# The second batch's chain: its products put behind the second-layer product of the moment and asked for later

## The chip, the cores and the metric

One core of a Trainium2 chip runs the whole kernel. The metric is the device time of one execution in microseconds. Three runs of the kernel before took 738.49, 745.61 and 740.89 us, median 740.89.

## What is computed

Four batches of 11,456 tokens of width 128 go through agent attention with 49 agents and then through a mixture of eight experts. Cut to what matters:

```python
a2k = sm(agents, k)                 # 49 agents over all keys, scaled softmax
agent_v = a2k @ v                   # per batch: 49 x 128
q2a = sm(q, agents)                 # every token over the 49 agents
x = q2a @ agent_v                   # attention output, 45824 x 128

xn = x / (norm(x) + 1e-6); en = expert_emb / (norm(expert_emb) + 1e-6)
logits = xn @ en.T / tau            # tau = 0.1
e = argmax(logits); gate_w = softmax(logits)[e]
out = gate_w * (relu(x @ w1[e]) @ w2[e])     # F = 1024 hidden units
```

## The kernel before, in words

Keys of a batch are read in blocks of 1,024 tokens, scored against the agents (tile `sp`), and the exponentials weight the values (`avp`). That gives the agents' values for the batch, and from them one expert that nearly all of the batch's tokens go to. With only 49 agent vectors behind every token, the kernel multiplies the agents' values into that expert's first layer once (`gp`), ranks the 1,024 hidden units, places the few that are not plainly linear into a small pair of weight matrices (`gh`, `gl` for the first layer, `w2p` for the second), and folds the rest into one linear matrix `lin`. Tokens that this doesn't cover are found by the products `vp` and mended later.

The piece from the agents' values to these small matrices is **the batch's chain**: `av_chain` (product `foldp`, its copy `lr` and `avT`, a sum over squares by the product `total<-avsq`, the router's weights `rp` rounded into `r_hi` and `r_lo`) and, started from it, `pick_expert` (product `key`, from which VectorE makes the expert's number `e0i`; SyncE reads it and loads the expert's weights `w1s` and `w2s`; ScalarE squares them, L688, and `total<-wsq` sums; then `gp`, the gates `gts`, the key of each hidden unit, the product `row`, ranks, the 0/1 matrices `sel`, the products `placed`, `linp` and `w2pp`, two products `mT` and `mB` for a maximum over partitions, the threshold `thr`).

While the chain of one batch goes on, the tokens of the batch before go through their layers, unit by unit: tokens are transposed on TensorE (`fTp`), scored (`sp`), routed (`rtp`), and in `route_group` get their gate `gs`. `ffn_mm1` is the first layer (`hp`, rectified into `hh`), and some ticks later `ffn_mm2` the second: it opens an accumulator `yp` with the linear part (`yp<-lin`, L1192) and adds the hidden units (`yp<-w2f`, L1201, or `yp<-w2p`, L1204 to L1206). `yp` has two accumulators; `ffn_out` frees one by writing `ot`, which is `yp` times `gs` (L1220, on VectorE). Scores, routing and the chain's products share another two (`pss`).

The kernel is written as generators: a `yield n` lets n half steps of other work be recorded before the generator goes on. A scheduler then sets each engine's order from dependencies and priorities. `in_place(last)` tells it that an instruction has to stand behind a named one. `y_last` is the last product of the second layer so far, so `in_place(y_last)` puts a product into TensorE's queue behind that. `gp`, `rp` and `placed` had it before. SyncE's queue keeps the order of the program, and the read of the expert's number holds it until the number is there.

Of the kernel before, what the change touches and what calls it, by code (L numbers as in the profile page):

```python
# [29 lines left out]
def kernel(ctx: ExitStack, tc: tile.TileContext, q, k, v, agents, emb, tau, w1, w2, out):  # L30
# [11 lines left out]
    AT = {2: {0: 0, 2: 1}, 3: {0: 0, 1: 1, 3: 2}}  # L42
    KEEP = 5
    LATE = 13

# [162 lines left out]

    def allmax(col, n, tag, psx, g, bufs=2):

        t_ = psx("mT")
        pe.transpose(out=t_[:n, :P], in_=col, identity=ident)
        mx = sm.tile([P, 1], F32, name="mTx", tag="mTx")[:n]
        dve.tensor_reduce(out=mx, in_=t_[:n, :P], axis=AX.X, op=ALU.max)
        yield g
        t_ = psx("mB")
        pe.matmul(out=t_[:, :n], lhsT=mx.broadcast_to([n, P]), rhs=ident[:n, :n], start=True, stop=True)
# [30 lines left out]

    def total(col, psx):

        s = psx("total")[:, :1]
        pe.matmul(out=s, lhsT=ones, rhs=col, start=True, stop=True)
        return s
# [294 lines left out]
    def av_chain(b, g):  # L548
        bt = batches[b]
        while not ready:  # L550
            yield 1
        psx = pss if ffn_at[0] else psy
        s = psx("foldp")
        fm = [(kb.x, kb.fold) for kb in bt.blks]
        for i, (x, m) in enumerate(fm):
            pe.matmul(out=s[:, :A], lhsT=x[:, :D], rhs=m, start=(i == 0), stop=(i == len(fm) - 1))
        for i, (x, m) in enumerate(fm):
            pe.matmul(out=s[:, LO : LO + A], lhsT=x[:, D : D + 1].broadcast_to([P, D]), rhs=m, start=(i == 0), stop=(i == len(fm) - 1))
        lr = sm.tile([P, A], F32, name="lr", tag="lr")
# [22 lines left out]
        if b == 0:  # L582
            rp, i = routing()
            p_last.append(i)
        bt.sg, bt.isg = yield from half_scale(total(sq, psx), 7, "sg")
        sg2 = sm.tile([P, 1], F32, name="sg2", tag="sg2")
# [41 lines left out]
    def pick_expert(b, g):  # L628
# [8 lines left out]
        sav = sm.tile([P, 1], F32, name="sav", tag="sav")  # L637
        dve.tensor_reduce(out=sav, in_=bt.avT[:, :A], axis=AX.X, op=ALU.add)
        key = psx("key")[:, :E]
        pe.matmul(out=key, lhsT=sav.broadcast_to([P, P]), rhs=enT, start=True, stop=True)  # L640
        km = sm.tile([P, 1], F32, name="km", tag="km")
# [45 lines left out]
        with in_place(q_last if b == 0 else h_last):  # L687
            act.activation(junk[0], w1s, AF.Square, accum_out=sq[0])  # L688
        s2, i2 = yield from half_scale(total(sq[0], psx), 2, "w1")
        sgw = sm.tile([P, 1], F32, name="sgw", tag="sgw")  # L690
# [7 lines left out]
        def second():  # L698

            act.activation(w2x[:, :, 0], w2s, AF.Square, accum_out=sq[1])  # L700
            s3, i3 = yield from half_scale(total(sq[1], psx), 6, "w2")
            yield g
            act.activation(w2x[:, :, 0], w2s, AF.Copy, scale=s3)
            if b > 0:
                pool.tensor_tensor(out=w2s, in0=w2s, in1=s3.unsqueeze(2).broadcast_to([P, NF, D]), op=ALU.mult)
                pool.tensor_tensor(out=w2x[:, :, 1], in0=w2s, in1=w2x[:, :, 0], op=ALU.subtract)
            return s3, i3
# [26 lines left out]
        if b > 0:  # L734
            s3, i3 = yield from second()
        yield g
        for h in range(2):
            t_ = psx("row")
            hs = slice(h * 512, h * 512 + 512)
            pe.matmul(out=t_, lhsT=ones, rhs=diag.rearrange("p c f -> p (c f)")[:, hs], start=True, stop=True)  # L740
            act.copy(row[:, hs], t_)
            yield g
# [24 lines left out]
        gmx = sm.tile([P, 2], F32, name="gmx", tag="gmx")  # L767
        yield 2 * g
        act.copy(gh, placed(0, FM))
# [19 lines left out]
        for h in (1, 0):  # L789
            vec.tensor_tensor(out=gts[:, :, h, :A], in0=ga, in1=mask.unsqueeze(2).broadcast_to([P, NF, A]), op=ALU.mult)  # L790
        yield 3 * g
        t_ = psx("linp")
        for c in range(NF):
            pe.matmul(out=t_[:, :D], lhsT=gts[:, c].rearrange("p h a -> p (h a)"), rhs=w2s[:, c],
                      start=(c == 0), stop=(c == NF - 1))
        ls_ = s3 if b == 0 else 1.0
# [6 lines left out]
        for f in range(0, NM, 2):  # L803
            t_ = psx("w2pp")
            nk = min(2, NM - f)
            for k_ in range(nk):
                for c in range(NF):
                    pe.matmul(out=t_[:, k_ * 2 * D : (k_ + 1) * 2 * D], lhsT=sel[:, c, (f + k_) * P : (f + k_ + 1) * P],
                              rhs=w2x[:, c].rearrange("p h d -> p (h d)"), start=(c == 0), stop=(c == NF - 1))
            (act.copy if f % 4 else dve.tensor_copy)(w2p[:, f : f + nk].rearrange("p f h d -> p (f h d)"), t_[:, : nk * 2 * D])  # L810
            yield g
# [7 lines left out]
        yield 1  # L819
        top = yield from allmax(gmx, 2, "gmxr", psx, 1)  # L820
        thr = sm.tile([P, 1], F32, name="thr", tag="thr")
# [4 lines left out]
        for c in range(NF):  # L826
            dve.tensor_scalar(sel[:, c, :FV], iotaf[:, :FV], rank[:, c : c + 1], sgn[:, c : c + 1], ALU.is_equal, ALU.mult)
            if c % 4 == 3:
                yield g
        yield 3 * g  # L830
        t_ = placed(0, FV)
# [845 lines left out]
```

## Time and profile before

| | before |
|---|---|
| median of three runs | 740.89 us |
| the profiled execution | 741.78 us |
| its span | 740.0 us |
| mean granted clock of TensorE | 0.972 |
| TensorE busy | 688.6 us |
| VectorE busy | 568.1 us |
| ScalarE busy | 475.6 us |
| GpSimd busy | 338.8 us |

The span is what the trace covers; the execution's own time is 1.8 us longer. Busy shares are means over the whole run, so the table alone tells only that TensorE has little room. Where the room lies, the windows and the timelines below show. The clock is given as a share of full speed.

### The profile page before, as it was taken

The page shows a single profiled execution, that of the slowest core. Times are in us where ns is not written, and L with a number is a line of the kernel's source. Part 1 is how long each engine was busy: PE and PEld are TensorE (multiplying, and loading weights), DVE is VectorE, ACT ScalarE, POOL GpSimd, SP SyncE. Part 2 cuts the span into 40 slices and gives each one's busy share as a digit, 9 for nine tenths or more (in the row PEclk, how much of TensorE's full clock was granted, in tenths as well). Part 3 has the DMA queues.
Part 4 walks back from the last instruction along what each step waited for, and adds up shares of the span by engine and source line. Part 5 has one row for each costly group of instructions (what it writes and reads, how often), then busy time and mean ns, then how long its engine had stood idle before and what let it go on. Part 6 is the DMA issues. An engine that isn't in the chain of part 4 may idle for free.

```text
span 740.0 us, 23507 instructions
## 1 busy us (share of the span) xinstructions
PE 688.6 (93%) x9416; PEld 574.9 (78%) x9416; DVE 568.1 (77%) x1499; ACT 475.6 (64%) x1161; POOL 338.8 (46%) x576
## 2 busy tenths in 40 slices
PE   8997889989978899999999889989999999999996
PEld 6886678867867788788888778878897776787675
DVE  4676887864457999988558998965658899789886
ACT  3436858667457757877758837865669447766772
POOL 5003401572245557655615836565638356255410
PEclk9998999999969999999999999999999999999998
DMA  8986239846389786598659439945452247223211
GB/s 329 278 306 215 94 73 249 187 137 197 95 205 342 154 199 166 148 279 214 160 158 268 112 67 253 287 124 159 135 172 94 81 87 194 62 60 115 61 45 64
DMA packets 157817, 122.59 MB, mean 166 GB/s; under 512 B 78727, under 2 KB 134105, under 8 KB 157707
## 3 DMA queue, kind: packets, MB, share of 16 engines
q1 hardware_dynamic: 144331, 97.44, 51.1%
q10 hardware_dynamic: 13120, 23.47, 9.1%
q8 instruction: 74, 1.21, 0.7%
q14 instruction: 36, 0.29, 0.1%
q0 software_dynamic: 256, 0.17, 0.1%
HBM read 79.14 MB, written 23.72 MB: 139 GB/s over the span
## 4 chain that ended last, share of the span: by engine, by line
PE 56%; DVE 23%; DMA 6%; ACT 5%; issue 4%; POOL 4%; SPq 0%; ACTq 0%; POOLq 0%; DVEq 0%
PE sp L430 8%; PE fTp L417 6%; PE avp L521 6%; PE hp L1168 4%; PE hp L1169 4%; PE yp L1192 3%; PE yp L1201 3%; DVE hh L1178 3%; PE yp L1204 3%; PE yp L1206 3%; PE yp L1205 3%; PE vp L1017 3%; DMA kt<-in_k_dram 2%; DVE ot L1220 2%; DMA xq<-in_q_dram,ix 1%
## 5 line engine op out<-in xcount | busy, mean ns | idle before, releaser
L1026 ACT ACTIVATE vp<-vp 128x512 f32<-128x512 f32 x191 | 112.3, 588 | 31.7 <-PE vp L1014 16.3
L1178 DVE SCALAR_TENSOR_TENSOR hh<-hp,hh 128x512 f16<-128x512 f32 (+1 forms) x147 | 98.4, 675 | 24.5 <-ACT hh L1177 23.9
L1204 PE MATMUL yp<-w2p,hh 128*128 128x128 f16 (+1 forms) x582 | 109.9, 220 | 0.0
L1205 PE MATMUL yp<-w2p,hh 128*128 128x128 f16 (+1 forms) x582 | 109.8, 220 | 0.0
L1206 PE MATMUL yp<-w2p,hh 128*128 128x128 f16 (+1 forms) x582 | 108.5, 220 | 0.0
L1177 ACT ACTIVATE hh<-hp 128x512 f16<-128x512 f32 (+1 forms) x147 | 85.1, 587 | 34.9 <-PE hp L1169 28.7
L430 PEld LDWEIGHTS sp<-aT_all,fT 128*64 128x64 f32 (+1 forms) x2400 | 83.7, 140 | 23.2 <-issue 11.5
L430 PE MATMUL sp<-aT_all,fT 128*64 128x49 f32 (+1 forms) x2400 | 97.6, 228 | 3.8 <-DVE qe L874 1.4
L1168 PE MATMUL hp<-tt,gh 128*128 128x512 f16 (+1 forms) x207 | 77.5, 377 | 4.3 <-DVE fT L420 2.4
L1169 PE MATMUL hp<-tt,gl 128*128 128x512 f16 (+1 forms) x207 | 77.8, 378 | 0.0
L965 POOL TENSOR_TENSOR nrm<-qq,half 128x16 f32<-128x16 f32 (+2 forms) x28 | 70.4, 2515 | 0.3
L884 POOL TENSOR_TENSOR e<-qe,e 128x392 f16<-128x392 f32 (+1 forms) x44 | 38.1, 866 | 68.0 <-ACT e L881 67.8
L1220 DVE TENSOR_TENSOR ot<-yp,gs 128x512 f32<-128x512 f32 (+1 forms) x92 | 61.1, 670 | 9.3 <-PE yp L1206 3.7
L1201 PE MATMUL yp<-w2f,hh 128*128 128x128 f32 (+1 forms) x456 | 66.7, 284 | 0.0
L1192 PE MATMUL yp<-lin,tt 128*128 128x128 f16 x720 | 63.3, 221 | 2.9 <-DVE w2p L810 1.4
L1204 PEld LDWEIGHTS <-hh 128*128 128x128 f16 (+1 forms) x582 | 57.6, 99 | 10.3 <-issue 0.5
L422 ACT COPY fT<-fTp 128x512 f32<-128x512 f32 (+1 forms) x87 | 48.6, 563 | 24.7 <-PE fTp L417 17.9
L1206 PEld LDWEIGHTS <-hh 128*128 128x128 f16 (+1 forms) x582 | 57.5, 99 | 8.1 <-issue 1.5
L1205 PEld LDWEIGHTS <-hh 128*128 128x128 f16 (+1 forms) x582 | 57.4, 99 | 5.8 <-issue 0.3
L1201 PEld LDWEIGHTS yp<-w2f,hh 128*128 128x128 f32 (+1 forms) x456 | 58.9, 194 | 2.9 <-issue 1.1
L926 POOL TENSOR_TENSOR rt<-rt 128x384 f32<-128x384 f32 (+1 forms) x48 | 40.5, 843 | 45.1 <-DVE rt L923 42.0
L417 PE MATMUL fTp<-ident,qt 128*128 128x128 f32 x360 | 57.0, 288 | 3.3 <-ACT fT L422 1.1
(373 smaller groups left out, 1786.3 us busy)
## 6 DMA issues: line engine op xcount, KB each, us to landing
kt<-in_k_dram SPq DMA_DIRECT2D x44, 512.0 KB, 6.6
vt<-in_v_dram SPq DMA_DIRECT2D x44, 512.0 KB, 6.2
qt<-in_q_dram SPq DMA_DIRECT2D x44, 512.0 KB, 5.5
out_dram<-ot ACTq DMA_DIRECT2D x88, 256.0 KB, 3.4
w1s<-in_moe_w_dram SPq DMA_DIRECT2D x8, 512.0 KB, 4.6
w2s<-in_moe_w_dram SPq DMA_DIRECT2D x8, 512.0 KB, 5.6
tt<-e SPq DMA_TRANSPOSE x44, 4.1
kt<-in_k_dram SPq DMA_DIRECT2D x4, 96.0 KB, 5.8
```

The lines of the kernel that those rows point to most:

```text
L417: pe.transpose(out=tp[:, c * p : (c + 1) * p], in_=src[:p, c0 + c, :], identity=ident[:p, :p])
L430: pe.matmul(out=s[h : h + w, c * A : (c + 1) * A], lhsT=xT[:, c * p + h : c * p + h + w], rhs=aT_all[:, b, :], start=True, stop=True, skip ...
L1026: act.activation(z[:p], z[:p], AF.Relu, scale=-1.0, accum_out=bt.vsum[:p, at : at + 1])
L1168: pe.matmul(out=hp[:, :m], lhsT=bt.gh[:, fs], rhs=tt, start=True, stop=False)
L1169: pe.matmul(out=hp[:, :m], lhsT=bt.gl[:, fs], rhs=tt, start=False, stop=True)
L1177: h_last[:] = [act.activation(hh[:, :m], hp[:, :m], AF.Relu)]
L1178: dve.scalar_tensor_tensor(out=hl[:, :m], in0=hp[:, :m], scalar=0.0, in1=hh[:, :m], op0=ALU.max, op1=ALU.subtract)
L1192: pe.matmul(out=yp[:p, c, :], lhsT=tc_, rhs=bt.lin[:, h], start=(c == 0 and h == 0), stop=False, skip_group_check=True)
L1201: y_last[:] = [pe.matmul(out=y, lhsT=hh[:, cs], rhs=bt.w2f[:, f], start=False, stop=last, skip_group_check=True)]
L1204: pe.matmul(out=y, lhsT=hh[:, cs], rhs=wh, start=False, stop=False, skip_group_check=True)
L1205: pe.matmul(out=y, lhsT=hh[:, cs], rhs=wl, start=False, stop=False, skip_group_check=True)
L1206: y_last[:] = [pe.matmul(out=y, lhsT=hl[:, cs], rhs=wh, start=False, stop=last, skip_group_check=True)]
```

## The change

A constant `EASY = 1` names the second batch. For that batch's chain alone, `foldp`, the three sums `total`, `key`, `row`, `linp`, `w2pp`, `mT` and `mB` are issued in place behind the second-layer product of the moment, and before several of them (and before `placed`) two or three more half steps are let pass. Nothing else is added, and no instruction is removed. Lines move down by up to 23.

```diff
+    EASY = 1
...
     def allmax(col, n, tag, psx, g, bufs=2, b=None):
...
+        with on_time(b):
+            pe.transpose(out=t_[:n, :P], in_=col, identity=ident)
...
-        yield g
+        yield g + (b == EASY)
...
+    def on_time(b):
+
+        return in_place(y_last) if b == EASY else nullcontext()
+
-    def total(col, psx):
+    def total(col, psx, b=None):
 
         s = psx("total")[:, :1]
-        pe.matmul(out=s, lhsT=ones, rhs=col, start=True, stop=True)
+        with on_time(b):
+            pe.matmul(out=s, lhsT=ones, rhs=col, start=True, stop=True)
...
         psx = pss if ffn_at[0] else psy
+        if b == EASY:
+            yield 2
         s = psx("foldp")
...
-        bt.sg, bt.isg = yield from half_scale(total(sq, psx), 7, "sg")
+        if b == EASY:
+            yield 3
+        bt.sg, bt.isg = yield from half_scale(total(sq, psx, b), 7, "sg")
...
+        if b == EASY:
+            yield 2
         key = psx("key")[:, :E]
-        pe.matmul(out=key, lhsT=sav.broadcast_to([P, P]), rhs=enT, start=True, stop=True)
+        with on_time(b):
+            pe.matmul(out=key, lhsT=sav.broadcast_to([P, P]), rhs=enT, start=True, stop=True)
...
-        s2, i2 = yield from half_scale(total(sq[0], psx), 2, "w1")
+        if b == EASY:
+            yield 3
+        s2, i2 = yield from half_scale(total(sq[0], psx, b), 2, "w1")
...
-            s3, i3 = yield from half_scale(total(sq[1], psx), 6, "w2")
+            if b == EASY:
+                yield 3
+            s3, i3 = yield from half_scale(total(sq[1], psx, b), 6, "w2")
...
-        yield g
+        yield g + 2 * (b == EASY)
         for h in range(2):
             t_ = psx("row")
...
-        yield 2 * g
+        yield 2 * g + 2 * (b == EASY)
         act.copy(gh, placed(0, FM))
...
-        yield 3 * g
+        yield 3 * g + 2 * (b == EASY)
         t_ = psx("linp")
...
-        top = yield from allmax(gmx, 2, "gmxr", psx, 1)
+        top = yield from allmax(gmx, 2, "gmxr", psx, 1, b=b)
...
-        yield 3 * g
+        yield 3 * g + 2 * (b == EASY)
         t_ = placed(0, FV)
```

`foldp`, `row`, `linp` and `w2pp` are wrapped in `on_time(b)` in the same way.

What moves is seen in each engine's order. **SyncE's queue around the read of the expert's number** of the second batch, before:

```order
L161 DMA qt<-in_q_dram 128x1024
L161 DMA kt<-in_k_dram 128x1024
L837 TENSOR_LOAD e0i
...
L840 DMA w1s<-in_moe_w_dram 128x1024
...
L841 DMA w2s<-in_moe_w_dram 128x8x128
L161 DMA qt<-in_q_dram 96x256
L481 DMA_TRANSPOSE kT<-ks 128x16x128
L161 DMA kt<-in_k_dram 128x1024
L161 DMA qt<-in_q_dram 128x1024
```

and with the change:

```order
L162 DMA qt<-in_q_dram 128x1024
L162 DMA kt<-in_k_dram 128x1024
L162 DMA qt<-in_q_dram 96x256
L489 DMA_TRANSPOSE kT<-ks 128x16x128
L162 DMA kt<-in_k_dram 128x1024
L860 TENSOR_LOAD e0i
...
L863 DMA w1s<-in_moe_w_dram 128x1024
...
L864 DMA w2s<-in_moe_w_dram 128x8x128
L162 DMA qt<-in_q_dram 128x1024
```

The last block of queries, the transpose of a key block and a load of keys, which stood behind the two loads of the expert's weights, now stand ahead of the read.

**TensorE from the folding product to the first batch's next second-layer product**, before (products that only repeat, and those of other work between, are left out):

```order
L556 MATMUL foldp<-fold,avx 128x49
L558 MATMUL foldp<-fold,avx 128x49
L252 MATMUL total<-avsq,ones 128x1
L640 MATMUL key<-enT,sav 128x8
...
L579 MATMUL rp<-enT,avT 128x8
L580 MATMUL rp<-avT 128x49
L430 MATMUL sp<-aT_all,fT 64x49 x32
L252 MATMUL total<-wsq_3572,ones 128x1
...
L682 MATMUL gp<-avT,w1s 128x49 x8
...
L1192 MATMUL yp<-lin,tt 128x128
...
L1201 MATMUL yp<-w2f,hh 128x128 x4
```

and with the change:

```order
L567 MATMUL foldp<-fold,avx 128x49
L569 MATMUL foldp<-fold,avx 128x49
...
L438 MATMUL sp<-aT_all,fT 64x49 x16
L656 MATMUL key<-enT,sav 128x8
L438 MATMUL sp<-aT_all,fT 64x49 x16
L260 MATMUL total<-avsq,ones 128x1
L590 MATMUL rp<-enT,avT 128x8
L591 MATMUL rp<-avT 128x49
...
L1215 MATMUL yp<-lin,tt 128x128
L1224 MATMUL yp<-w2f,hh 128x128 x4
L260 MATMUL total<-wsq_3617,ones 128x1
```

`key` now stands inside the scores and ahead of `total<-avsq`; `total<-wsq` stood ahead of `gp` and of `yp<-lin`, and stands behind that second-layer product now, with `gp` behind it.

**VectorE from the folding product's copy `lr` to the output `ot`** of the first batch, before:

```order
L560 TENSOR_SCALAR lr<-foldp 128x49
L561 RECIPROCAL lr<-lr 128x49
L564 TENSOR_TENSOR avT<-foldp,lr 128x2x49
L638 TENSOR_REDUCE sav<-avT 128x1
...
L646 TENSOR_REDUCE e0i<-ko 128x1
L647 TENSOR_SCALAR e0i<-e0i 128x1
L923 TENSOR_TENSOR rt<-rtp,qe 128x392
...
L242 TENSOR_SCALAR hsc<-ksq 128x1
L989 RECIPROCAL gs<-el 128x16
...
L1220 TENSOR_TENSOR ot<-yp,gs 128x512 x2
L476 SCALAR_TENSOR_TENSOR ks<-kt,hsc,ks 128x8x128
```

and with the change:

```order
L245 TENSOR_SCALAR hsc<-ksq 128x1
...
L249 TENSOR_SCALAR hiv<-hsc,kbias 128x1
L484 SCALAR_TENSOR_TENSOR ks<-kt,hsc,ks 128x8x128
L571 TENSOR_SCALAR lr<-foldp 128x49
L572 RECIPROCAL lr<-lr 128x49
L946 TENSOR_TENSOR rt<-rtp,qe 128x392
L984 TENSOR_REDUCE rmx<-rtg 128x16
L575 TENSOR_TENSOR avT<-foldp,lr 128x2x49
L651 TENSOR_REDUCE sav<-avT 128x1
...
L662 TENSOR_REDUCE e0i<-ko 128x1
L663 TENSOR_SCALAR e0i<-e0i 128x1
...
L1012 RECIPROCAL gs<-el 128x16
L1243 TENSOR_TENSOR ot<-yp,gs 128x512 x2
```

The scaled copy `ks` of a key block with its scale steps `hsc` now stands ahead of `lr`, and two routing steps stand between `lr` and `avT`; before, `ks` stood behind `ot`.

## Rows read from the trace of the kernel before

**Rows 1.** The page's first part: busy us, share of the span, instructions.
```profile
PE 688.6 (93%) x9416; PEld 574.9 (78%) x9416; DVE 568.1 (77%) x1499; ACT 475.6 (64%) x1161; POOL 338.8 (46%) x576
```

**Rows 2.** Windows: length; busy us (instructions) of PE, PEld, DVE, ACT, POOL; PEclk, DMA, GB/s.
```profile
202.36:224.00 21.64, 17.03 (x152) 15.24 (x151) 12.55 (x46) 11.57 (x25) 7.76 (x13) 0.68 0.81 213
...
211.53:252.04 40.51, 35.08 (x371) 30.18 (x371) 29.95 (x72) 30.70 (x62) 15.76 (x21) 0.87 0.99 260
...
260.00:330.00 70.00, 68.06 (x1031) 58.50 (x1031) 66.03 (x179) 50.41 (x136) 42.41 (x76) 1.00 0.73 190
...
310.00:400.00 90.00, 89.99 (x1300) 78.78 (x1297) 64.48 (x175) 64.66 (x159) 40.68 (x62) 1.00 0.77 203
...
483.00:486.50 3.50, 3.13 (x29) 2.40 (x30) 0.93 (x2) 1.91 (x5) 1.57 (x5) 0.56 0.62 123
```

**Rows 3.** Timeline of TensorE, 202 to 221 us: start, length, instruction, [idle before].
```profile
204.37 0.38 PE L252 MATMUL total<-avsq,ones 128*128 128x1 f32 x2 [1.46 <-ACT lr L574]
...
211.53 0.38 PE L252 MATMUL total<-wsq,ones 128*128 128x1 f32 x2 [1.69 <-ACT sel L688]
...
214.27 3.54 PE L682 MATMUL gp<-avT,w1s 128*128 128x49 f32 x16
...
219.25 1.03 PE L1192 MATMUL yp<-lin,tt 128*128 128x128 f16 x8
```

**Rows 4.** Timeline of SyncE's queue, 187 to 228 us.
```profile
189.16 0.38 SPq L161 DMA_DIRECT2D kt<-in_k_dram  x1
...
206.79 0.36 SPq L840 DMA_DIRECT2D w1s<-in_moe_w_dram  x1
```

**Rows 5.** Timeline of VectorE, 200 to 222 us.
```profile
202.94 0.21 DVE L560 TENSOR_SCALAR lr<-foldp 128x49 f32<-128x49 f32 x1 [1.44 <-PE foldp L558]
...
205.79 0.15 DVE L647 TENSOR_SCALAR e0i<-e0i 128x1 int32<-128x1 int32 x1
...
217.65 0.15 DVE L242 TENSOR_SCALAR hsc<-ksq 128x1 int32<-128x1 int32 x1 [2.19 <-ACT ks L466]
...
217.72 0.24 DVE L989 RECIPROCAL gs<-el 128x16 f32<-128x16 f32 x1
...
218.34 1.29 DVE L1220 TENSOR_TENSOR ot<-yp,gs 128x512 f32<-128x512 f32 x2
...
219.54 1.28 DVE L476 SCALAR_TENSOR_TENSOR ks<-kt,hsc,ks 128x1024 f16<-128x1024 f32 x1
```

**Rows 6.** Timelines of ScalarE and GpSimd, 208 to 221 us.
```profile
210.33 1.06 ACT L688 ACTIVATE sel<-w1s 128x1024 f16<-128x1024 f32 x1 [2.69 <-DMA w1s<-in_moe_w_dram]
...
215.90 0.22 POOL L986 TENSOR_TENSOR el<-el,la 128x16 f32<-128x16 f32 x1
```

**Rows 7.** Timeline of TensorE, 250 to 282 us.
```profile
252.04 1.91 PE L763 MATMUL placed<-sel,gt 128*128 128x256 f16 x16 [1.39 <-DVE sel L755]
...
259.13 2.05 PE L794 MATMUL linp<-w2s,gts 128*128 128x128 f32 x16
...
262.58 1.92 PE L808 MATMUL w2pp<-w1s,sel 128*128 128x256 f16 x16
...
264.34 0.61 PE L1192 MATMUL yp<-lin,tt 128*128 128x128 f16 x8
...
281.37 0.22 PE L1204 MATMUL yp<-w2p,hh 128*128 128x128 f16 x1
```

**Rows 8.** Timeline of VectorE, 250 to 273 us.
```profile
251.48 1.81 DVE L755 TENSOR_SCALAR sel<-iotaf,rank 128x256 f16<-128x256 f16 x7
...
265.54 3.97 DVE L827 TENSOR_SCALAR sel<-iotaf,rank,sgn 128x320 f16<-128x320 f16 x7
...
269.43 0.68 DVE L810 CAST w2p<-w2pp 128x512 f16<-128x512 f32 x1
```

More of the change, by code (lines that the diff above doesn't have):

```diff
@@ L207, in now_run, with allmax @@
                 return s.value
-    def allmax(col, n, tag, psx, g, bufs=2):
+    def allmax(col, n, tag, psx, g, bufs=2, b=None):
         t_ = psx("mT")
-        pe.transpose(out=t_[:n, :P], in_=col, identity=ident)
+        with on_time(b):
+            pe.transpose(out=t_[:n, :P], in_=col, identity=ident)
         mx = sm.tile([P, 1], F32, name="mTx", tag="mTx")[:n]
         dve.tensor_reduce(out=mx, in_=t_[:n, :P], axis=AX.X, op=ALU.max)
-        yield g
+        yield g + (b == EASY)
         t_ = psx("mB")
-        pe.matmul(out=t_[:, :n], lhsT=mx.broadcast_to([n, P]), rhs=ident[:n, :n], start=True, stop=True)
+        with on_time(b):
+            pe.matmul(out=t_[:, :n], lhsT=mx.broadcast_to([n, P]), rhs=ident[:n, :n], start=True, stop=True)
         r = sm.tile([P, n], F32, name="pm", tag=tag, bufs=bufs)
@@ L552, in av_chain @@
         psx = pss if ffn_at[0] else psy
+        if b == EASY:
+            yield 2
         s = psx("foldp")
         fm = [(kb.x, kb.fold) for kb in bt.blks]
[L555 to L558, printed above, removed]
+        with on_time(b):
+            for i, (x, m) in enumerate(fm):
+                pe.matmul(out=s[:, :A], lhsT=x[:, :D], rhs=m, start=(i == 0), stop=(i == len(fm) - 1))
+            for i, (x, m) in enumerate(fm):
+                pe.matmul(out=s[:, LO : LO + A], lhsT=x[:, D : D + 1].broadcast_to([P, D]), rhs=m, start=(i == 0), stop=(i == len(fm) - 1))
         lr = sm.tile([P, A], F32, name="lr", tag="lr")
@@ L638, in pick_expert @@
         dve.tensor_reduce(out=sav, in_=bt.avT[:, :A], axis=AX.X, op=ALU.add)
+        if b == EASY:
+            yield 2
         key = psx("key")[:, :E]
-        pe.matmul(out=key, lhsT=sav.broadcast_to([P, P]), rhs=enT, start=True, stop=True)
+        with on_time(b):
+            pe.matmul(out=key, lhsT=sav.broadcast_to([P, P]), rhs=enT, start=True, stop=True)
         km = sm.tile([P, 1], F32, name="km", tag="km")
@@ L739, in pick_expert @@
             hs = slice(h * 512, h * 512 + 512)
-            pe.matmul(out=t_, lhsT=ones, rhs=diag.rearrange("p c f -> p (c f)")[:, hs], start=True, stop=True)
+            with on_time(b):
+                pe.matmul(out=t_, lhsT=ones, rhs=diag.rearrange("p c f -> p (c f)")[:, hs], start=True, stop=True)
             act.copy(row[:, hs], t_)
@@ L790, in pick_expert @@
             vec.tensor_tensor(out=gts[:, :, h, :A], in0=ga, in1=mask.unsqueeze(2).broadcast_to([P, NF, A]), op=ALU.mult)
-        yield 3 * g
+        yield 3 * g + 2 * (b == EASY)
         t_ = psx("linp")
-        for c in range(NF):
-            pe.matmul(out=t_[:, :D], lhsT=gts[:, c].rearrange("p h a -> p (h a)"), rhs=w2s[:, c],
-                      start=(c == 0), stop=(c == NF - 1))
+        with on_time(b):
+            for c in range(NF):
+                pe.matmul(out=t_[:, :D], lhsT=gts[:, c].rearrange("p h a -> p (h a)"), rhs=w2s[:, c],
+                          start=(c == 0), stop=(c == NF - 1))
         ls_ = s3 if b == 0 else 1.0
@@ L805, in pick_expert @@
             nk = min(2, NM - f)
[L806 to L809, printed above, removed]
+            with on_time(b):
+                for k_ in range(nk):
+                    for c in range(NF):
+                        pe.matmul(out=t_[:, k_ * 2 * D : (k_ + 1) * 2 * D], lhsT=sel[:, c, (f + k_) * P : (f + k_ + 1) * P],
+                                  rhs=w2x[:, c].rearrange("p h d -> p (h d)"), start=(c == 0), stop=(c == NF - 1))
             (act.copy if f % 4 else dve.tensor_copy)(w2p[:, f : f + nk].rearrange("p f h d -> p (f h d)"), t_[:, : nk * 2 * D])
```

## The prediction

> **What bounds the kernel now.** I began with the busy time of each engine: TensorE works 688.6 us of a span of 740.0 us [rows 1], so only some 51 us of the run are open to any reordering on it. Then I read the busy time and granted clock by stretches, to see where those 51 us lie. In the piece that the change touches they lie thick: from the folding product of the second batch's chain to the end of the low clock (202.36 to 224.00) TensorE is busy 17.03 of 21.64 us and its mean granted clock is 0.68 [rows 2], which is a mix of its two levels, 1.2 and 2.4 GHz. So 4.6 us of idle and, at a loss of 0.32 x 21.64, up to 6.9 us of slow clock stand there. From 310 to 400 us TensorE is busy without a gap (89.99 of 90.00 us [rows 2]); what the chain wins or loses before that is therefore handed on to the end, and only the idle of the stretch up to there can soak up a loss: 70.00 - 68.06 = 1.94 us between 260 and 330 [rows 2].
>
> The timeline of TensorE names the waits [rows 3]. The sum over the squared agent vector waits 1.46 us for ScalarE, the sum over the squared expert weights (total<-wsq) 1.69 us for ScalarE's Square. Behind that the first-layer product gp takes 3.54 us at the low clock, and the second-layer product yp<-lin of the first batch begins at 219.25. SyncE explains the second wait: nothing leaves its queue from the load of keys at 189.16 until the expert's weights at 206.79, since the read of the expert's number stands at the head of its queue [rows 4]. VectorE writes that number at 205.79 [rows 5], the weights are squared from 210.33 for 1.06 us [rows 6].
>
> **The change, part by part.** No product is added or taken away; the price is in who waits for whom.
>
> *First stretch, up to yp<-lin.* On SyncE three entries now go ahead of the read of the number. Their buffers are free early, so they leave soon after 189.16 and the next block of keys is there before the chain asks. Its scaled copy on VectorE (1.28 us in the row at 219.54) with three small steps, which stood behind the second-layer output, now stands ahead of lr, the first copy out of the folding product [rows 5]. So lr slips from 202.94 to about 205.0 (estimate: 1.28, three steps of about 0.15, and the rest a wait for ScalarE's half of that copy). The routing's steps now stand between lr and the expert's number, and the key product asks two half steps later: I walk the number from 205.94 (205.79 + 0.15) to about 209.4, the weights' issue from 206.79 to 210.3, and the end of the Square (210.33 + 1.06 = 211.39 before) keeps its distance of 4.6 us from the issue: 214.9.
>
> The sum over those weights no longer stops TensorE, since it stands behind yp<-lin. But yp<-lin needs a free accumulator, hence the output ot, and ot needs the gate gs. ScalarE's second rounding of the router, the one that gs comes from, now stands behind the Square. From 214.9 the steps to ot are a rounding of about 0.3, its remainder 0.3, a sum 0.3, two GpSimd steps (the second 0.22 in its row), the reciprocal 0.24 and one ot, 0.65 as half of 1.29 [rows 5, 6]: 2.3 us and five handovers of about 0.15 by my estimate, so yp<-lin at about 218. TensorE has run out of work ahead of it at about 211.5. **This is my central point: the wait moves from the chain's product to the second-layer product, and does not go.** Against 219.25 that is 1.25 us early, but 2.0 us of products (total<-wsq and gp at full clock, 3.54 / 2 + 0.2) that lay ahead now lie behind. The low clock lasted 4.7 us beyond yp<-lin, until 224.00, 2.4 us lost; after a long stop I take the row 483.00 to 486.50, clock 0.56, 1.5 us lost [rows 2]. So -1.25 + 2.0 - 0.9, near 0. Bounds: 0 against -10 if the stop does not come (first rival).
>
> What shows that the stop can come is VectorE at 217.65: the scale of a key block waited there 2.19 us for ScalarE, and gs, whose input was ready at 216.12 on GpSimd, ran only behind it at 217.72 [rows 5, 6]. A ready step stood 1.6 us behind one that was not. The Trainium skill, "PSUM — Partial Sum Buffer", section "Engine vs sequencer instructions", says that the queues of VectorE and ScalarE are strict first-in first-out; by it a delayed Square holds up all behind it, which speaks against this change, and if a ready step could pass, the stop would shrink and the time would be the first rival's, 731 us. This trace agrees by the 1.6 us.
>
> *Second stretch, to w2pp.* The sum over the weights is asked for at about 220.5 and the gates follow about 10 us later than before. What TensorE has to do from there to the next stop: before, 211.53 to 252.04 was 35.08 us busy at a mean clock of 0.87 [rows 2]; less 40.51 x 0.13 = 5.3 that is 30 us of work, and the order puts some 4 us more between. So TensorE reaches the yp<-lin ahead of placed at about 220.5 + 34 + 2.5 of small waits = 257. This yp<-lin needs two outputs ot of 1.29 us in all, which in the change stand on VectorE behind the eight selections, the mask and a routing gate. The last seven selections ended at 253.29 (251.48 + 1.81) [rows 8]; 10 us later, with 1.29 for ot and 1.7 for the routing between, that is 266. VectorE may have caught up part of the 10 us. With no lateness the stop is 0 and TensorE goes on at 257; I take the middle, 261.5. Before, it stood at its yp<-lin at 264.34, but with placed, linp and w2pp done (1.91 + 2.05 + 1.92 = 5.9 us [rows 7]), which in the change are still to come. Term: 261.5 - 264.34 + 5.9 = +3.1; bounds -1.4 (257) and +7.6 (266). The wait of placed for VectorE, 1.39 us in the same rows, is inside this.
>
> *Third stretch, to the first product with the new second-layer weights.* Before, w2pp ends at 264.5, the copy w2p is made at 269.43 and used at 281.37: 11.3 us of slack [rows 7, 8]. In the change only about 3.3 us of other products stand between, while VectorE has seven selections (3.97) and the copy (0.68) to do there, and needed 5.6 us for them before (264.5 to 270.11). New wait: 2.3 us, bounds 0 (if VectorE makes the selections before w2pp ends) and 2.3 plus nothing, since the copy itself needs no more.
>
> *After it.* VectorE and TensorE both are nearly full up to 330; TensorE can make up at most its idle there, 1.94 us [rows 2]; I take it whole.
>
> **Sum:** 0 + 3.1 + 2.3 - 1.9 = +3.5 us. The profiled execution of before took 741.78 us, 0.9 more than the median of the three runs, 740.89; so 745.3 against the one and **744.4 us** against the other, which is the forecast. With the bounds of the second and third term it reaches from 737 (-1.4 + 0 - 1.9 = -3.3) to 749 (+8.0).
>
> **The rivals.** *It pays.* The stop of yp<-lin does not come: VectorE passes the key block's copy quicker, the expert's number is not late, and the products of the chain simply find their operands ready, which is what more time between asking and use gives. For it speaks that the three chain waits of 1.46, 1.69 and 1.39 us are real [rows 3, 7] and that the low clock follows them. The price: of the 4.6 us idle and 6.9 us of low clock of the first stretch [rows 2], 11.5 in all, up to 2.9 come back as short waits of the scores for VectorE's routing steps, and 1.4 of placed go: -10.0, 731 us. Against it: the weights are asked for later, not earlier, and the gate hangs on them by ScalarE's order.
>
> *VectorE becomes the bound* (the other side). The 10 us by which the gates are late are not caught up, because VectorE's selections, copies and outputs come as one block: the second stop lasts to 266, TensorE's clock falls once more behind it (1.5), the copy of w2p costs its 2.3 and nothing is made up since VectorE stays full: 0 + 7.6 + 1.5 + 2.3 = +11.4, 752 us. It decides from the point at which the second stop is longer than about 7 us. For it: VectorE was 66.03 of 70.00 us busy between 260 and 330 already [rows 2]; against it: the row product, which comes between, is reached by TensorE not much later than before by the order, so much of the 10 us may be hidden.
>
> *It does nothing that counts:* the waits trade places one for one and the stretch ends where it did, 741 us. It lies inside the forecast's own range.
>
> **How the numbers follow.** A difference below 1% (7.4 us) is what a measurement of this kernel can't tell from none: 733.5 and 748.3 are the marks. The forecast, moved waits, 0.42; nothing that counts, 0.06; it pays, 0.24; VectorE the bound, 0.28. The last two have their own spread: of the first rival's chance some 0.21 lies below 733.5, of the second's 0.25 above 748.3; the forecast's upper end adds 0.06 to the slower side. So faster 0.22, same 0.47, slower 0.31. For 8 in 10 the range takes in half of either rival: 731 to 753.
>
> **What would show it.** Right: TensorE's waits in this stretch name yp<-lin behind VectorE's ot, not total<-wsq behind ScalarE; one low-clock spell behind it; the expert's weights leave SyncE at about 210; the gates come about 10 us later; a second wait of yp<-lin near 257 to 266; a short wait of the first product with the new weights for w2p. Wrong for the forecast, right for the first rival: idle below 3 us between the folding product and gp, and no low clock there. Wrong by size: an expert's number at 206, or a second stop beyond 7 us. Wrong altogether: a loss that lies behind 330 us, where I take TensorE to run as before, or a change of the later batches, whose chains the change does not name.

## The result, and the profile after

| | median, us | range, us | runs |
|---|---|---|---|
| before | 741.38 | 738.49 to 745.61 | 9 |
| changed | 749.1 | 746.13 to 755.48 | 9 |

The estimated ratio is 1.0112, with a 95% interval of 1.0084 to 1.0141: the change makes the kernel slower by 1.1%. The forecast was 744.4 us with a range of 731 to 753. The time lies in the range, 4.7 us above the forecast and between it and the rival with 752. It also lies just beyond 748.3, the mark from which the prediction calls a kernel slower, at a chance of 0.31. The profiled execution of the changed kernel took 748.77 us (before 741.78), its span is 747.0 us (740.0), TensorE's mean granted clock 0.966 (0.972). The page's first part answers to [rows 1]:

```profile
PE 687.6 (92%) x9416; PEld 575.0 (77%) x9416; DVE 566.2 (76%) x1499; ACT 477.7 (64%) x1161; POOL 341.0 (46%) x576
```

TensorE does the same 9416 products and is busy 1.0 us less, so it is idle 8.0 us longer; what the slower clock costs is inside the busy time. The two places where the stops were forecast come first. On TensorE's timeline of the changed kernel (start, length, instruction, the idle before it and what ended that) the two waits of the chain's sums [rows 3] and the wait of `placed` [rows 7] are gone, and `yp<-lin` waits twice for the output `ot`:

```profile
206.94 0.38 PE L260 MATMUL total<-avsq,ones 128*128 128x1 f32 x2
...
214.78 1.01 PE L1215 MATMUL yp<-lin,tt 128*128 128x128 f16 x8 [5.09 <-DVE ot L1243]
...
217.40 0.43 PE L260 MATMUL total<-wsq,ones 128*128 128x1 f32 x2
...
221.74 1.88 PE L698 MATMUL gp<-avT,w1s 128*128 128x49 f32 x16
...
258.23 1.01 PE L1215 MATMUL yp<-lin,tt 128*128 128x128 f16 x8 [4.67 <-DVE ot L1243]
262.15 1.39 PE L784 MATMUL placed<-sel,gt 128*128 128x256 f16 x8
...
281.31 0.22 PE L1227 MATMUL yp<-w2p,hh 128*128 128x128 f16 x1
```

`gp` takes 1.88 us where it took 3.54, since the low clock now lies ahead of it. The windows of the changed kernel (columns as in [rows 2]) show the clock behind each stop, and two later places:

```profile
201.25:224.00 22.75, 15.18 (x204) 14.14 (x202) 13.01 (x45) 9.68 (x25) 8.95 (x15) 0.77 0.76 227
...
214.78:218.00 3.22, 3.22 (x26) 3.21 (x26) 0.69 (x2) 0.28 (x1) 0.48 (x2) 0.50 1.02 366
...
258.23:263.00 4.77, 4.77 (x31) 3.95 (x31) 4.00 (x8) 1.30 (x3) 4.35 (x10) 0.51 1.15 225
260.00:330.00 70.00, 69.12 (x998) 59.28 (x997) 60.95 (x169) 48.18 (x127) 40.62 (x73) 0.98 0.71 178
310.00:400.00 90.00, 86.55 (x1219) 74.77 (x1217) 60.11 (x161) 60.64 (x151) 35.99 (x57) 0.98 0.78 190
340.00:345.00 5.00, 3.84 (x36) 2.77 (x36) 1.59 (x5) 1.50 (x5) 1.04 (x2) 0.66 0.99 282
405.11:420.02 14.91, 10.38 (x118) 8.82 (x117) 11.58 (x32) 11.68 (x27) 11.65 (x17) 0.77 0.83 177
```

A clock of 0.50 is the lower level, 1.2 GHz, throughout: behind each stop there is one such spell. Yet the stretch as a whole is level. The first product with the new second-layer weights stands at 281.31 against 281.37 [rows 7]. The difference opens further on, as fixed points of both TensorE timelines tell:

| point on TensorE | before, us | changed, us | later by | gained on the row above |
|---|---|---|---|---|
| `foldp` (second batch's chain) | 202.36 | 201.25 | -1.1 | |
| `yp<-w2p` | 281.37 | 281.31 | -0.1 | +1.0 |
| `mT` of the greatest key | 303.55 | 302.16 | -1.4 | -1.3 |
| `foldp` (third batch's chain) | 377.93 | 381.77 | +3.8 | +5.2 |
| `total<-wsq` (third) | 399.94 | 405.11 | +5.2 | +1.3 |
| `row` (third) | 410.21 | 420.02 | +9.8 | +4.6 |
| end of the span | 740.0 | 747.0 | +7.0 | -2.8 |

Two steps of the table carry the loss, and neither lies in the chain that the change names. **The first** is between 303 and 378 us. Before, TensorE is busy 89.99 of 90.00 us from 310 to 400 [rows 2]; now 86.55, and from 340 to 345 its clock is 0.66. There it waits for the token that the first batch gathers by an indirect transfer:

```profile
341.16 0.30 PE L1282 MATMUL sqT<-ident,xq 128*128 128x128 f32 x1 [3.45 <-DMA xq<-in_q_dram,ix]
```

The idle time from 310 to 400 is this one wait (90.00 - 86.55 = 3.45); with the slow clock behind it, 0.34 x 5.00 = 1.7, it makes nearly all of the 5.2 us of the step. GpSimd's timeline shows that the transfer is issued at 332.46. Its index `ix` is written on VectorE at 329.53, 1.9 us later than before (327.65), and a norm of 2.93 us now stands ahead of the issue:

```profile
329.29 2.93 POOL L988 TENSOR_TENSOR nrm<-qq,half 128x16 f32<-128x16 f32 x1
...
332.46 1.30 POOL L1273 DMA_INDIRECT xq<-in_q_dram,ix  x1 [0.18 <-DVE qe L897]
```

Before, the transfer was issued at 327.96, ahead of that norm, and `sqT` waited for nothing (GpSimd's timeline, then TensorE's):

```profile
327.96 1.30 POOL L1250 DMA_INDIRECT xq<-in_q_dram,ix  x1 [0.70 <-DVE ix L1329]
...
334.30 2.94 POOL L965 TENSOR_TENSOR nrm<-qq,half 128x16 f32<-128x16 f32 x1
```

```profile
338.04 0.33 PE L1259 MATMUL sqT<-ident,xq 128*128 128x128 f32 x1
```

**The second** is the third batch's chain from `total<-wsq` to `row`: 14.91 us against 10.27. TensorE's work in it is the same (8.09 us at clock 1.00 before; 10.38 x 0.77 = 8.0 now), so 4.53 - 2.18 = 2.35 us more is idle time and the rest slower clock. Most of the idle time is a wait of the values' product `vp` for VectorE's least value `vmin`:

```profile
415.08 0.58 PE L1040 MATMUL vp<-vm,tt 128*128 128x256 f16 x2 [3.72 <-DVE vmin L1046]
```

VectorE's timeline names what stands ahead of `vmin`, the negated key `nkey` of 1.86 us:

```profile
412.57 1.86 DVE L751 TENSOR_SCALAR nkey<-key 128x8 f32<-128x8 f32 x1
414.35 0.68 DVE L1046 TENSOR_REDUCE vmin<-vp 128x8 f32<-128x512 f32 x1
```

In the kernel before the same two steps stand the other way round, and its `vp` waits 1.91 (TensorE's row and window, then VectorE's):

```profile
407.56 0.38 PE L1017 MATMUL vp<-vm,tt 128*128 128x256 f16 x2 [1.91 <-DVE vmin L1023]
```

```profile
399.94:410.21 10.27, 8.09 (x119) 6.98 (x117) 9.97 (x28) 9.42 (x24) 8.46 (x10) 1.00 1.17 266
```

```profile
406.82 0.68 DVE L1023 TENSOR_REDUCE vmin<-vp 128x8 f32<-128x512 f32 x1
407.42 1.48 DVE L731 TENSOR_SCALAR nkey<-key 128x8 f32<-128x8 f32 x1
```

The change names neither step. The scheduler makes one order for the whole program, so products asked for later in one place can shift steps in another; why it exchanged just these two was not looked into.

### The profile page after: what moved, and what is told of

The parts are those of the page before. It is cut to its first block, busy times and chain, and to the rows that moved or that the text cites. A ratio compares the mean times of both kernels' runs of the same rounds, so it can differ in the third digit from the quotient of the medians.

```text
span 747.0 us, 23500 instructions
## 1 busy us (share of the span) xinstructions
PE 687.6 (92%) x9416; PEld 575.0 (77%) x9416; DVE 566.2 (76%) x1499; ACT 477.7 (64%) x1161; POOL 341.0 (46%) x576
## 5 line engine op out<-in xcount | busy, mean ns | idle before, releaser
L1224 PE MATMUL yp<-w2f,hh 128*128 128x128 f32 (+1 forms) x456 | 70.3, 291 | 0.0
L1224 PEld LDWEIGHTS yp<-w2f,hh 128*128 128x128 f32 (+1 forms) x456 | 61.7, 201 | 3.3 <-issue 1.1
L1215 PEld LDWEIGHTS <-tt 128*128 128x128 f16 x720 | 49.7, 100 | 18.4 <-issue 11.6
```

Source lines behind the costliest of these rows:

```text
L1215: pe.matmul(out=yp[:p, c, :], lhsT=tc_, rhs=bt.lin[:, h], start=(c == 0 and h == 0), stop=False, skip_group_check=True)
L1224: y_last[:] = [pe.matmul(out=y, lhsT=hh[:, cs], rhs=bt.w2f[:, f], start=False, stop=last, skip_group_check=True)]
```

## Experiments

**The theory** after these traces: the stops that the change moves cost nothing net; the loss is the late gather and the exchanged `nkey`. **The rivals**: the moved stops carry it (in the first half of the chain, or in the second), or the half steps alone would have done the same without the place behind the second layer.

**Only the half steps, no placing.**

```diff
-        return in_place(y_last) if b == EASY else nullcontext()
+        return nullcontext()
```

> The changed kernel with its extra half steps but without the new placing behind the second-layer product. The order on every engine is that of the changed kernel but for one product: the sum over the expert's squared weights stands ahead of yp<-lin again. My theory, that the half steps alone move the waits and the placing does nothing: time of the changed kernel, ratio to before 1.008 to 1.014, and the stop of 5.09 us of yp<-lin turns up as a wait of about 5 us of that sum for ScalarE. Rival, that the placing behind the second layer costs the time: ratio 0.997 to 1.003.

Measured: 753.49 us, ratio 1.0192 (1.0158 to 1.0225). That is above the range of the theory (1.008 to 1.014) and far from the rival. Without the placing TensorE's order differs from the changed one in one position, `total<-wsq` ahead of `yp<-lin` instead of behind; on VectorE the steps that follow from that sum stand ahead of `gs` and `ot`. TensorE's timeline in this run:

```profile
216.79 0.59 PE L260 MATMUL total<-wsq,ones 128*128 128x1 f32 x2 [0.88 <-ACT sel L704]
...
219.84 1.01 PE L1215 MATMUL yp<-lin,tt 128*128 128x128 f16 x8 [2.45 <-DVE ot L1243]
```

The first stop stands in two parts, 0.88 and 2.45 us, and a second one of 5.01 us follows as in the changed kernel. So the half steps make the loss and the placing gives some of it back: the intervals of 1.019 and 1.011 do not touch. Why one position is worth that much the trace does not tell: its execution took 748.8 us, the quickest of the six.

**The first half of the chain alone** (`foldp`, both sums up to the weights, `key`), and **the second half alone** (the second sum over weights to `mB`).

```diff
-        yield g + 2 * (b == EASY)
+        yield g
...
-            s3, i3 = yield from half_scale(total(sq[1], psx, b), 6, "w2")
+            s3, i3 = yield from half_scale(total(sq[1], psx), 6, "w2")
```

(and so at the other places of the second half; the other kernel has the same at those of the first)

> The change for the first half of the chain alone (foldp, the sum over the agents' squares, key, the sum over the first weights); row and all behind it as before. Theory: the first stop of yp<-lin, about 5 us, stays, the second one, 4.67 us, shrinks below 2; by 282 us the kernel is level with before or 2 us ahead, and what is lost later depends on the order behind it: ratio 1.000 to 1.007. Rival, that the late asking in the first half carries the whole loss: ratio 1.010 or more.

> The change for the second half of the chain alone (the sum over the second weights, row, placed, linp, w2pp, mT and mB); the first half as before. Theory, two separate stops: the first stop of yp<-lin goes (wait below 1 us at 214 to 220 us), the second one, 4.67 us, stays or shrinks to 2; level with before by 282 us, and the total depends on the order behind it: ratio 0.996 to 1.007. Rival, that the late asking of the second half carries the loss: ratio 1.009 to 1.014 with level arrival at 205 to 225 us.

Measured: 747.58 us, ratio 1.0106 (1.0072 to 1.0141), and 748.93 us, ratio 1.0076 (1.0047 to 1.0105). Both are above the range of their theory, and the first lies where its rival has it, that the late asking of the first half carries the loss. But each half alone costs most of what both cost together, so the loss is no sum of two halves. In the first-half kernel the first stop is 3.78 us and the second 0.24; in the second-half kernel the chain's waits are back (1.46 and 1.97) and the only stop of `yp<-lin` is

```profile
262.14 0.61 PE L1207 MATMUL yp<-lin,tt 128*128 128x128 f16 x8 [2.22 <-DVE ot L1235]
```

From each kernel's own `foldp` to the `mT` of the greatest key it took, in one execution of each, 101.19 us (before), 100.91 (changed), 103.52 (first half), 105.32 (second half). The full change is the quickest of the four in its own stretch and no quicker at the end. That speaks against the moved stops as the cause.

**The Square behind the second rounding**, to free `ot` from the weights.

```diff
-        with in_place(q_last if b == 0 else h_last):
+        while b == EASY and not hasattr(bt, "r_hi"):
+            yield 1
+        with in_place(q_last if b == 0 else [bt.hi_i] if b == EASY else h_last):
```

> The changed kernel with ScalarE's second rounding of the router's weights ahead of the Square of the expert's weights (the Square waits to be recorded until it is). Theory: the gate of the routing no longer hangs on the expert's weights, so the first stop of yp<-lin falls from 5.09 us to below 2 and the low clock behind it goes or shortens; gain 3 to 5 us up to there, ratio to before 1.003 to 1.008. Rival, that VectorE bounds the stretch: the first stop shrinks and the second grows by as much, ratio 1.009 to 1.014.

Measured: 744.02 us, ratio 1.0033 (1.0008 to 1.0058). The time is as expected and the reason is not: the first stop is 5.50 us, no shorter, since ScalarE's exponential `ex`, a step on the way to the gate, still stands behind the Square, as it did in the changed kernel. What came out better is the order far behind: `nkey` takes 0.17 us there and the third batch's `row` is 2.9 us later than before, counted from each kernel's `foldp`, instead of 10.9. `sqT` still waits 3.06 us for the gather. I had changed one step and moved others.

**Eight half steps more between the first batch's gather and its use.**

```diff
-        yield 18
+        yield 18 + 8 * (b == 0)
```

> The changed kernel with eight more half steps between the gather of the first batch's stray token and the product that turns it. Theory, that half of the loss arises behind 330 us where TensorE waits 3.45 us for this gather and then runs 1.7 us' worth at the low clock: both go, gain 3 to 5 us, ratio to before 1.004 to 1.008. Rival, that the loss arises in the two stops of yp<-lin before 282 us and this wait only shows it: ratio 1.009 to 1.014.

Measured: 745.78 us, ratio 1.006 (1.003 to 1.009). `sqT` waits for nothing, while the stops of `yp<-lin` are 6.07 and 5.02 us. But the order behind it moves too, and `nkey` is short here as well, so this run does not separate the two causes. It also shows that other orders lose elsewhere: neither of the two places stands out in its trace and `row` is only 1.2 us later than before, counted from `foldp`, yet the kernel is 0.6% slower; in the execution traced, the slowest of its 12, the loss lies behind `row`.

**The turning product takes another operand** (the identity for the gathered token, which leaves out part of the first batch's answer; the gather is still made); **`nkey` of the third batch on ScalarE**; **both**.

```diff
-            pe.transpose(out=t_[:, :P], in_=xq, identity=ident)
+            pe.transpose(out=t_[:, :P], in_=xq if other is None else other, identity=ident)
```

```diff
-        dve.tensor_scalar(nkey, key, -1.0, None, ALU.mult)
+        if b == 2:
+            act.activation(nkey, key, AF.Copy, scale=-1.0)
+        else:
+            dve.tensor_scalar(nkey, key, -1.0, None, ALU.mult)
```

> The changed kernel, in which the turning product for the first batch's stray token reads the identity and not the gathered token, so that it waits for no gather (that token's answer is left out). TensorE's, VectorE's, ScalarE's and SyncE's orders are otherwise those of the changed kernel. Theory: the wait of 3.45 us and the low clock behind it (1.7 us) are part of the loss, and 3 to 5 us come back: ratio to before 1.004 to 1.008. Rival, that they only show a loss made before 282 us: ratio 1.009 to 1.014.

> The changed kernel with one small step of the third batch's chain (nkey, the negated keys) on ScalarE, out of VectorE's queue, where it took 1.86 us ahead of vmin; all other orders as in the changed kernel. Theory: TensorE's wait for vmin falls from 3.72 us to below 2.5, so the low clock that follows it (clock 0.77 between 405 and 420 us, 3.4 us lost) goes as well: gain 3 to 5 us, ratio 1.004 to 1.008. Rival, that the stretch is bound by something else and the wait only changes its name: gain below 1 us, ratio 1.010 to 1.014.

> Both of the former in one kernel (the first batch's stray answer is left out). Theory: the loss of the changed kernel lies in these two places alone, since it was level with before at 282 us; 6 to 9 us come back, ratio to before 0.998 to 1.003. Rival, that one place hands its loss to the next: gain no larger than the larger of the two alone, ratio 1.004 or more.

Measured: 751.83 us, ratio 1.0101 (1.0074 to 1.0129); 747.65 us, 1.0058 (1.0029 to 1.0087); 747.67 us, 1.0069 (1.0039 to 1.0098). The second is as the theory says: TensorE's, GpSimd's and SyncE's orders are those of the changed kernel, VectorE's too but for `nkey`, and `vp` waits 1.95 us, about as before:

```profile
410.54 0.38 PE L1043 MATMUL vp<-vm,tt 128*128 128x256 f16 x2 [1.95 <-DVE vmin L1049]
```

The first is a miss: the wait went, the time did not. The trace of that run (GpSimd, VectorE, TensorE) shows why:

```profile
344.32 0.20 POOL L123 MEMSET xq<- 128x128 f32 x1 [3.58 <-DMA xq<-in_q_dram,ix]
```

```profile
346.99 0.25 DVE L1012 RECIPROCAL gs<-el 128x16 f32<-128x16 f32 x1 [4.30 <-POOL vt L123]
```

```profile
348.12 0.58 PE L1191 MATMUL hp<-tt,gh 128*128 128x512 f16 x1 [3.31 <-DVE hh L1201]
```

GpSimd clears the buffer for the next gather and waits for the landing of this one; behind the clearing stand GpSimd's steps for a gate, behind the gate the reciprocal, `hh` and TensorE. Without the wait of its own TensorE only met the same transfer three engines later. The edit had itself moved that clearing: with `sqT` no longer reading the tile, it stands ahead of `e` and `el` on GpSimd, where in the changed kernel it stands behind them, at 341.52. So this run tells where a late gather can be met, and not what the wait at `sqT` costs. In the third kernel it stood 4.54 us at `hp` in the same way, so its ratio, 1.0069 where 0.998 to 1.003 was expected, cannot show the sum of two cures.

**The first batch's gather left out altogether** (the answer of its stray token is computed from the cleared tile, so that part of the output is not the reference's); **the same with `nkey` on ScalarE**; and a control, **`nkey` on ScalarE in the kernel before**.

```diff
+        if skip:
+            return xq
         pool.indirect_dma_start(out=xq, out_offset=None
...
-        xq = gather(ix)
+        xq = gather(ix, b == 0)
```

> The changed kernel without the gather for the first batch's stray token (its tile is cleared and not filled, so that token's answer is left out). Up to that place the order is that of the changed kernel; behind it some products move. Unlike the run in which only the turning product was freed, nothing waits for the gather any more, GpSimd included. Theory, that the late gather costs 1 to 5 us depending on when it lands: ratio to before 1.003 to 1.009. Rival, that the gather's wait is hidden in the mean and the loss lies in the third batch's chain alone: ratio 1.010 to 1.014.

> The former kernel with nkey of the third batch on ScalarE as well (the stray answer of the first batch left out). Theory, two places behind 330 us carry the loss: ratio 0.997 to 1.004. Rival, that the loss comes from before 282 us, or that the third chain's loss stays whatever is freed: ratio 1.006 or more.

> A control: the kernel before with nkey of the third batch on ScalarE. There vmin stood ahead of nkey on VectorE already and TensorE waited 1.91 us for it. Theory, that the step costs TensorE time only where it stands ahead of vmin: ratio 0.998 to 1.002, so that what the same edit gave the changed kernel is a part of its loss. Rival, that the step is worth as much in any order: ratio 0.993 to 0.996.

| | median, us | ratio | interval |
|---|---|---|---|
| changed | 749.1 | 1.0112 | 1.0084 to 1.0141 |
| `nkey` moved | 747.65 | 1.0058 | 1.0029 to 1.0087 |
| gather left out | 744.31 | 1.0019 | 0.9991 to 1.0048 |
| both | 741.08 | 0.9999 | 0.9968 to 1.003 |
| before with `nkey` moved | 741.74 | 0.9999 | 0.9971 to 1.0026 |

With both taken away the loss is gone, and the same move of `nkey` is worth nothing in the kernel before. Without the gather alone more came back than its theory had (1.003 to 1.009). Here is the decisive reading: in the kernel with both, the two moved stops are still there, 3.88 and 4.72 us. TensorE's timeline of it:

```profile
214.67 1.01 PE L1218 MATMUL yp<-lin,tt 128*128 128x128 f16 x8 [3.88 <-DVE ot L1246]
...
258.18 1.01 PE L1218 MATMUL yp<-lin,tt 128*128 128x128 f16 x8 [4.72 <-DVE ot L1246]
...
407.14 0.38 PE L1043 MATMUL vp<-vm,tt 128*128 128x256 f16 x2 [2.05 <-DVE vmin L1049]
```

From `foldp` it takes 101.17 us to the `mT` of the greatest key (before 101.19), 176.20 to the third batch's `foldp` (175.57; changed 180.52) and 208.80 to its `row` (207.85; changed 218.77). Its windows are as full as those of before, 90.00 of 90.00 us from 310 to 400:

```profile
310.00:400.00 90.00, 90.00 (x1283) 78.54 (x1279) 62.86 (x171) 63.64 (x158) 41.09 (x62) 1.00 0.82 205
400.00:410.00 10.00, 7.95 (x118) 6.97 (x117) 8.32 (x26) 10.00 (x26) 8.47 (x8) 1.00 1.08 249
```

The kept traces narrow the share of each. From the `mT` of the greatest key to the third batch's `foldp` it took 79.61 us in the changed kernel, and 80.23 and 81.12 in the two whose GpSimd waits for the gather. In the same order of products it took 75.33 with `nkey` moved, where the gather landed sooner and `sqT` waited 0.70 us, and 75.04 with the half steps alone, where `sqT` did not wait for it; without the gather 75.03, twice; before 74.38. From `total<-wsq` to `row` it took 14.04 to 15.04 us in the four executions with `nkey` ahead of `vmin`, and 9.92, 10.84 and 12.48 in the three with it on ScalarE. So in an execution that meets it the late gather costs some 4 to 6 us and the exchanged step some 2 to 5. The 10.27 us of before flatter it: in its order the same stretch took 11.81 and 11.73 in two other executions (`nkey` moved in the kernel before, and the last experiment below), in which the low clock followed the same wait of 1.9 us, so that some 1.5 of the 4.6 us in the table differ from one execution to the next.

What this does not settle is the share of each in the medians. Leaving the gather out also moves the order of products from 337 us on; with the gather gone but `nkey` in place `vp` still waits 3.82 us in the trace, and the whole is only 0.2% slower than before in the median, but the execution traced is the slowest of its 12, at 749.54 us; the intervals of neighbouring rows of the table overlap. The kernel before was not run without that gather; its `sqT` waited for nothing. Open also: the two stops of `yp<-lin` were not taken away with all else in place, which would need a third accumulator, and why the order exchanges just `vmin` and `nkey`.

**The kernel before, with four half steps more behind the second batch's gather.** In it TensorE waits 2.12 us for that gather at 483.37, where the clock falls [rows 2]:

```profile
483.37 0.47 PE L1259 MATMUL sqT<-ident,xq 128*128 128x128 f32 x1 [2.12 <-DMA xq<-in_q_dram,ix]
```

```diff
-        yield 18
+        yield 18 + 4 * (b == 1)
```

> The kernel before with four more half steps between the gather for the second batch's stray token and the product that turns it; there the kernel before waits 2.1 us at 483 us and runs at the low clock for 3 us after it. Theory, that a late gather costs its wait and the low clock: gain 2 to 4 us, ratio 0.995 to 0.998, faster than both kernels. Rival, that TensorE makes it up behind it, or that the order that moves takes it back: ratio 0.999 to 1.004.

Measured: 738.99 us, ratio 0.9951 (0.9921 to 0.9981), quicker than both kernels. The order of products behind 477 us moves too, so the gain need not be the wait's alone. The wait in this run is 0.81, and the clock is whole:

```profile
483.64 0.33 PE L1259 MATMUL sqT<-ident,xq 128*128 128x128 f32 x1 [0.81 <-DMA xq<-in_q_dram,ix]
```

```profile
480.00:490.00 10.00, 9.19 (x139) 7.53 (x138) 5.62 (x15) 7.98 (x22) 8.79 (x16) 1.00 0.55 141
```

## Why the prediction was right, and where it was not

*The wait moves and does not go*: right. Both stops stand at `yp<-lin`, behind `ot`, with one low-clock spell behind each, and `total<-wsq` waits for nothing. The changed kernel's SyncE and VectorE rows bear the reason out in part only: the expert's weights leave at 207.09, not 210.3, and the number is there at 206.24 (206.09 + 0.15), not 209.4.

```profile
207.09 0.36 SPq L863 DMA_DIRECT2D w1s<-in_moe_w_dram  x1
```

```profile
200.69 1.28 DVE L484 SCALAR_TENSOR_TENSOR ks<-kt,hsc,ks 128x1024 f16<-128x1024 f32 x1 [1.03 <-ACT ks L478]
201.90 0.20 DVE L571 TENSOR_SCALAR lr<-foldp 128x49 f32<-128x49 f32 x1
...
206.09 0.15 DVE L663 TENSOR_SCALAR e0i<-e0i 128x1 int32<-128x1 int32 x1
```

The copy of the key block does stand ahead of `lr`, as the order said, but it ran earlier, from 200.69, so `lr` was not held. A number at 206 was the sign that I had named for a wrong size. Hence the Square ended at 211.76 (210.70 + 1.06) where I had 214.9, and ScalarE's rows show what stands behind it:

```profile
210.70 1.06 ACT L704 ACTIVATE sel<-w1s 128x1024 f16<-128x1024 f32 x1 [2.14 <-DMA w1s<-in_moe_w_dram]
211.75 0.28 ACT L610 ACTIVATE r_hi<-rp,sg 128x49 f16<-128x49 f32 x1
...
212.11 0.30 ACT L1002 ACTIVATE ex<-lga 128x128 f32<-128x128 f32 x1
```

One link of the reason was wrong. The prediction lets the gate `gs` come from the rounding `r_hi`; but that is the second batch's router, and the first batch's gate comes from `ex`, which stands two steps behind it in the same queue. Nor is the Square the larger part of the stop: the operand of `ex` was there at 210.63 (GpSimd's `lga`, 210.22 + 0.41), so by these rows the Square held `ex` for about 1.5 us, an estimate, and the rest of the 5.09 us is what the gate's other steps take after TensorE has run out of work.

The stop of 5.09 us ends at 214.78 instead of 218, while TensorE ran out of work at 209.69 (214.78 - 5.09) and not at 211.5. What the rounding waits for was there by 208.82 (VectorE's `r_lo`, 208.59 + 0.23), and though ScalarE stood idle up to the Square at 210.70 it did not run; it starts as the Square ends. The Trainium skill, "PSUM — Partial Sum Buffer", section "Engine vs sequencer instructions", has the queues of ScalarE and VectorE strictly first-in first-out, and these rows agree.

*The three terms* (0, +3.1, +2.3, less 1.9 of idle): too high together. By `yp<-w2p` the kernels are level, where the sum had +5.4 before the idle time was used up; counted from `foldp` it is 1.0 us. The gates came 3.7 us later, not 10 (`gts` 223.92 against 220.19), so the second stop ended at 258.23, not 261.5, near the lower bound of 257; it is as long as forecast (4.67 us for 261.5 - 257), and TensorE came to it 3.4 us sooner. The third wait, 2.3 us for `w2p`, did not come: the copy was done at 280.20 and the product stood at 281.31, behind other work. Of the 1.94 us of idle 0.88 was left (70.00 - 69.12).

*The step that failed* is the one behind 330 us, "where I take TensorE to run as before": I took the stretch from 310 on, busy 89.99 of 90.00 us, as a thing that would hand on what it is given. It was full only because a gather and a few steps of VectorE were in time, and a change elsewhere can move them. The prediction named such a loss behind 330 us as the sign of being wrong altogether, gave it no term in the sum and no chance. In the traces the gather's wait with its low clock (3.45 + 1.7 us) and the longer way from `total<-wsq` to `row` (4.64 us) stand in its place; with both taken away the loss of 7.7 us between the medians is gone (ratio 0.9999). That the number fell into the range is luck in part: terms that were too high made up for part of the one that was missing. The rival that VectorE becomes the bound of the second stretch, at 752 us, has the nearer time for its size but not its mechanism: its sign was a second stop beyond 7 us.

## What to carry to other kernels

Where a planner sets the order, list every instruction that changes its place in the whole program, not only near the edit, and ask of each transfer and each short step that moved whether it had slack; a window that is 100% busy says nothing of how close its waits are. A wait that is taken out at one engine is only gone if no engine behind waits for the same event: take out the event itself, and look at what else the edit moved, to learn its price. Runs of one order in which a transfer happens to land sooner or later show that price too. And a stop of 5 us need not be a loss: compare where the stretch ends.

## What the runs showed of the hardware

A step of VectorE on 128x8 numbers took 0.17 us or 1.86 us, as a GpSimd product over 128x1024 had begun behind it or ahead of it. In the run with eight more half steps, VectorE and GpSimd:

```profile
411.16 0.17 DVE L751 TENSOR_SCALAR nkey<-key 128x8 f32<-128x8 f32 x1
```

```profile
411.20 1.90 POOL L749 TENSOR_TENSOR sel<-ident,key 128x1024 f32<-128x1024 f32 x1 [0.85 <-DVE key L747]
```

In the changed kernel the same step began at 412.57 and ended at 414.43, and GpSimd's product lay around it:

```profile
412.19 2.21 POOL L749 TENSOR_TENSOR sel<-ident,key 128x1024 f32<-128x1024 f32 x1 [0.30 <-DVE r_hi L607]
```

The short step ends with the long one, at 414.40; before, 407.42 + 1.48 = 408.90 against 406.98 + 1.90 = 408.88 on GpSimd. On ScalarE the step took 0.21 us. Two more steps of this size in the changed kernel's chain end with a GpSimd step that began ahead of them: `pw` at 408.44 (407.09 + 1.35) with `gt` at 408.41 (406.70 + 1.71), and `key` at 411.70 (410.42 + 1.28) with `w2s` at 411.67 (409.78 + 1.89). Not every step is held: the copy `fT` out of PSUM, begun at 409.82 beside that same `w2s`, took 0.67 us. I have this from rows alone and ran nothing made to show it. The Trainium skill, "SBUF — State Buffer", section "SBUF: two separate sides", has a rule for it: a port pair that VectorE and GpSimd share is locked by whichever begins first, a GpSimd step or a VectorE step of certain kinds (in a 2-port mode, or, against a GpSimd step that reads SBUF, with two inputs from there), for its whole instruction, and the other blocks. These rows agree for VectorE as the one that waits; in which mode the step ran they do not tell.

The gather of 128 rows landed 8.6 us after its issue in the changed kernel, and 5.8 us after it in the kernel with `nkey` moved; with one order up to there TensorE waited 3.45 and 0.70 us for it.
